# One core: ALiBi and mask move from VectorE into the score matmul group, and float64 weights convert without a clamp

## The chip, the core and the metric

One core of a Trainium2 chip runs the whole program. The metric is the device time of one execution in microseconds; the kernel before took 464.65 us (median of 3 runs, 463.22 to 468.41). The engines are TensorE (PE, with its weight loads as PEld), VectorE (DVE), ScalarE (ACT), GpSimd (POOL) and SyncE (SP), which issues the DMAs. Each works through its own queue in the order in which the program wrote it.

## What is computed

Three blocks follow one another, all in float32 (weights come partly as float64 bits):

```python
# attention: 2 x 8 heads, 768 positions, head width 64, n_global = 8, n_local = 96
scores = scale * q @ k.T
is_global = pos[None, :] < n_global;  is_local = (rel >= 0) & (rel < n_local)     # rel = query - key
dist = where(is_global & ~is_local, n_local, abs(rel))
scores = where(is_global | is_local, scores - slopes[h] * dist, -1e9)
a = exp(scores - scores.max(-1));  a = a / (a.sum(-1) + 1e-9);  x = a @ v         # heads side by side: [2, 768, 512]
# first mixture
theta = x @ w_theta
y = w_tok_r @ (x * cos(theta)) + w_tok_i @ (x * sin(theta));  u = x + y
x2 = u + max(u @ w_ch, 0)
# second mixture
h = max(x2 @ w_in, 0);  c = conv3(h, conv_w) along the positions
out = (h * sigmoid(c)) @ w_out
```

A query tile of 128 positions needs only its own tile of keys, the local keys before it, and the 8 global keys.

## The kernel before, in words

Large products are made from a high part in fp32r and a low part (the rest), three matmuls for one. `hi` (L79 on ScalarE, L83 on VectorE) rounds to the high part, `lo` (L87) makes the low part, `mm` (L90) is every matmul. For the scores, Q high and Q low are two stationary operands against one K whose upper half holds its own low part, so each query tile has two score matmuls.

**Attention loop.** `run_fast` runs 48 groups, three per head, each of a pair of query tiles, as a software pipeline. In step j the program writes `scores` of group j, `softmax` of j-1 (L299), `exps` of j-2 (L308), `transposes` of j-3 (L317), `evacuate` of j-4 (L79, ScalarE) and `pv` of j-5; then come, by step, `table` (L269), the normalisation, the high and low parts of the next head's K and Q, and transposes of finished heads (L416). A query tile's scores are 256 columns: 120 local keys before it, 8 global keys and its own 128; the first tile of a head has only its own 128. Scores of a pair lie in one PSUM bank; the tag S has two such banks. `softmax` is one custom VectorE instruction for each tile: it adds the head's table T (distance times slope, masked entries huge) to the scores in PSUM, scales, writes the sum to an SBUF buffer `sS` and gives the row minimum, which a second small instruction reads out. `exps` then works in place on `sS`, so the bank is free once the custom instructions are done. `table` makes T from the distance table `Dt` anew for each head, two instructions.

**Weights.** Every weight tile is a job of six items in `Net.weight`: load (L117, on SP's queue, into one of two buffers `wst`), `f64_a` (L95, ScalarE, absolute value of the upper words), `f64_b` (L100 clamps in float, L101 shifts and masks in integers, both VectorE), `f64_c` (L107, L108, VectorE), then the high part (L79, ScalarE) and the low part (L87, VectorE). `advance` lists the items of neighbouring jobs in the order low part of n-3, `f64_a` of n-1, `f64_b` and `f64_c` of n-2, load of n, high part of n-2. The loop takes one item per step up to step 32 and three from then on; later stages take up to twelve between groups of matmuls. The jobs are 4 of w_theta (512 columns), 24 of w_tok (384), then 4 of w_ch, 8 of w_in and 8 of w_out (512).

**After attention.** `theta` of batch 0 runs within the last third of the loop, 6 matmuls of 512 columns a step. `reduce_theta` (L456 to L459) scales it on ScalarE, rounds it with the magic number in one VectorE instruction (L458) and subtracts (L459); 12 tiles in all. `trig` (L466 to L472) makes the sine and cosine parts. Then `tail` runs the token matmuls, w_ch, w_in with the convolution and gate, and w_out.

`begin` computes the distance table, the high and low parts of the first head, and a flag that chooses between `run_fast` and a general arm; the scores of group 0 need only the first half of those parts.

Of the kernel before, what the change touches and what calls it, by code (L numbers as in the profile page):

```python
# [21 lines left out]
P = 128  # L22
# [3 lines left out]
NH = B * H  # L26
NG = 8
NPREV = P - NG
# [14 lines left out]
def f32_of_bits(b):  # L43
    return float(np.array([b], np.uint32).view(np.float32)[0])


F64_LOW = f32_of_bits(0x38000000)
F64_HIGH = f32_of_bits(0x47EFFFFF)


class Net:
# [41 lines left out]
    def f64_a(self, w, t):  # L93

        self.nc.scalar.activation(t.bitcast(F32), w[:, 1 : w.shape[1] : 2].bitcast(F32), AF.Abs)  # L95

    def f64_b(self, w, t):

        nc = self.nc
        nc.vector.tensor_scalar(t.bitcast(F32), t.bitcast(F32), F64_LOW, F64_HIGH, op0=ALU.max, op1=ALU.min)  # L100
        nc.vector.tensor_scalar(t, t, 3, 0x3FFFFFFF, op0=ALU.logical_shift_left, op1=ALU.bitwise_and)  # L101

    def f64_c(self, w, t):

        nc = self.nc
        lo, hi = w[:, 0 : w.shape[1] : 2], w[:, 1 : w.shape[1] : 2]
        nc.vector.scalar_tensor_tensor(t, lo, 29, t, op0=ALU.logical_shift_right, op1=ALU.bitwise_or)  # L107
        nc.vector.scalar_tensor_tensor(t, hi, -(1 << 30), t, op0=ALU.bitwise_and, op1=ALU.bitwise_or)  # L108
# [89 lines left out]
class Attention:  # L198


    def __init__(self, net, xs):
# [9 lines left out]
        self.sS = [a2[:, 715 + 512 * i : 715 + 512 * i + 512] for i in range(3)]  # L211
        self.pt = [a0[:, w + vw : w + vw + 512], a1[:, w + vw : w + vw + 512], a2[:, 2251:2763]]
        self.T = [a2[:, 2763:3019], a1[:, SLOT - P :]]
        self.qk = [n.head["qk0"], n.slot("a3", [P, 2 * S + NT * KW], F32R, "qk1")]
# [36 lines left out]
def split_q(net, st, qk, eh, el):  # L251
    q = st[:, 0:S]
    net.hi(eh, qk[:, 0:S], q)
    net.lo(el, qk[:, S : 2 * S], q, qk[:, 0:S])


class FastAttention(Attention):
# [15 lines left out]

    def scores(self, j):
        i, tp = divmod(j, 3)
        net = self.net
        Q, K = self.Q(i), self.K(i)
        sp = net.bank("S", 2)
        for u in range(2):
            t = 2 * tp + u  # L280
            if t == 0:
                o, r = sp[:, P : 2 * P], K[:, 0:P]
            else:
                o, r = sp[:, 256 * u : 256 * u + 256], K[:, KW * (t - 1) + NG : KW * t + P]
            for a in range(2):
                net.mm(o, Q[:, a, t * P : t * P + P], r, a == 0, a == 1)
        self.state[j] = {"sp": sp}

    def softmax(self, j):
        i, tp = divmod(j, 3)  # L290
        nc, net, s = self.nc, self.net, self.state[j]
        sS = self.sS[j % 3]
        nm = net.small.tile([P, 2], F32, tag="nm", name=net.uid("nm"), bufs=3)
        rng = []
        for u in range(2):
            t0 = tp == 0 and u == 0
            c = slice(256 * u + (P if t0 else 0), 256 * u + 256)
            rng.append(c)
# [4 lines left out]
        s["exp"] = (sS, rng, nm)  # L303

    def exps(self, j):
        sS, rng, nm = self.state[j]["exp"]
        for u in range(2):
            self.nc.scalar.activation(sS[:, rng[u]], sS[:, rng[u]], AF.Exp, bias=nm[:, u : u + 1], scale=-1.0)  # L308

    def transposes(self, j):  # L310
# [4 lines left out]
        for u, a in self.chunks(tp):  # L315
            c = slice(256 * u + P * a, 256 * u + P * a + P)
            self.nc.tensor.transpose(pt[:, c], sS[:, c], net.head["ident"])  # L317
# [23 lines left out]
class GeneralAttention(Attention):  # L341


    def unit(self, i, t, o):
# [18 lines left out]
        for hf in range(2):  # L363
# [5 lines left out]
            nc.scalar.activation(s[:, HALF * hf : HALF * hf + HALF], sp[:, 0:HALF], AF.Copy, scale=0.125)  # L369
# [17 lines left out]
class Mix:  # L387
# [64 lines left out]
    def reduce_theta(self, th, out):  # L452
# [3 lines left out]
        nc.scalar.activation(out, th, AF.Copy, scale=1.0 / TWO_PI)  # L456
        yield
        nc.vector.tensor_scalar(t, out, MAGIC, -MAGIC, op0=ALU.add, op1=ALU.add)  # L458
        nc.vector.tensor_tensor(out, out, t, op=ALU.subtract)  # L459

    def trig(self, b, t, r, z, em, eh, el):
# [5 lines left out]
        nc.scalar.activation(r, r, AF.Sin, scale=TURN)  # L467
# [132 lines left out]
    def tail(self, early):  # L600
# [94 lines left out]
        self.wch = [wc[:, c] for c in range(3)] + [wr[:, 0]]  # L695
        src = n.io["w_ch"].rearrange("(c p) n -> c p n", p=P)
# [24 lines left out]
        for step in (n.f64_a, n.f64_b, n.f64_c):  # L721
            step(n.head["cwb"], n.head["cwt"])
# [56 lines left out]
def run_fast(tc, net):  # L779
# [13 lines left out]
    mix.alloc_xTs()  # L793
    NJ = 3 * NH
# [20 lines left out]
    for j in range(NJ + LAG_N + 3):  # L815
# [6 lines left out]
        if tp == 0 and i < NH:  # L822
            att.table(i)
# [108 lines left out]
def begin(nc, io, net, small, head):  # L932
# [9 lines left out]
    cwb = small.tile([P, 2 * NF * 3], I32, name="cwb")  # L942
    nc.sync.dma_start(cwb, io["conv_w"].bitcast(I32))

    R = scratch[:, STAGE : STAGE + 384]
    Dt = small.tile([P, 384], F32, name="Dt")
    nc.gpsimd.iota(R[:, 0:NPREV], pattern=[[-1, NPREV]], base=NPREV, channel_multiplier=1, allow_small_or_imprecise_dtypes=True)
    nc.gpsimd.iota(R[:, NPREV:P], pattern=[[1, NG]], base=0, channel_multiplier=0, allow_small_or_imprecise_dtypes=True)
# [71 lines left out]
```

## Time and profile before

| | |
|---|---|
| median of 3 runs | 464.65 us (463.22 to 468.41) |
| profiled execution, span | 463.6 us |
| busy: PE / PEld / DVE / ACT | 411.5 / 380.5 / 383.3 / 217.6 us |
| instructions | 6488 |
| last chain by engine: DVE / PE / DMA / ACT | 46% / 37% / 7% / 4% |

Busy time is the union of an engine's instructions; a matmul's end is modelled and its record holds the pipeline's latency, so a busy PE can have room left. The granted clock is given as a share of 2.4 GHz: 1.00 is 2.4 GHz and 0.50 is 1.2 GHz. In the rows below L is a line of the kernel before.

### The profile page before, as it was taken

To read this page: it belongs to the slowest core of one execution; us is meant where nothing else is said; L and a number is where in the kernel's file an instruction comes from. 1 tells how busy PE (TensorE), PEld (TensorE's weight loads), DVE (VectorE), ACT (ScalarE), POOL (GpSimd) and SP (SyncE) were. 2 spreads that over 40 slices of the span, in tenths; PEclk is the share of its full clock that TensorE was granted. 3 is DMA by queue.
4 is the path that set the end of the run, shared out by engine and by line. 5 is a ranking of instruction groups with operands and counts; after the bars stand their busy time and mean duration, and the time that the engine had idled before them with its cause. 6 is when DMAs were issued, how large, how long until landed. Compare 5 with 4: busy or idle time off the path is not lost.

```text
span 463.6 us, 6488 instructions
## 1 busy us (share of the span) xinstructions
PE 411.5 (89%) x2376; PEld 380.5 (82%) x2376; DVE 383.3 (83%) x854; ACT 217.6 (47%) x420; POOL 1.4 (0%) x10
## 2 busy tenths in 40 slices
PE   3788778889988999899876999769999999999995
PEld 2777778777877799899765999759999999888885
DVE  5899998999999998898677898899999999991000
ACT  4767765866657731641322323373465454540000
POOL 1000000000000000000000000000000000000000
PEclk9999978999999999999999999979999999999999
DMA  6865554555231002202444343322311000003111
GB/s 231 308 197 201 175 167 152 187 172 171 66 101 35 1 0 69 69 2 68 108 130 125 92 136 105 123 92 60 122 47 47 0 1 0 1 0 136 47 45 52
DMA packets 14296, 44.52 MB, mean 96 GB/s; under 512 B 1840, under 2 KB 2352, under 8 KB 14256
## 3 DMA queue, kind: packets, MB, share of 16 engines
q1 hardware_dynamic: 14256, 44.03, 29.6%
q8 instruction: 20, 0.33, 0.3%
q14 instruction: 20, 0.16, 0.1%
HBM read 40.88 MB, written 3.15 MB: 95 GB/s over the span
## 4 chain that ended last, share of the span: by engine, by line
DVE 46%; PE 37%; DMA 7%; ACT 4%; issue 3%; SPq 0%; ACTq 0%; DVEq 0%
PE O L90 11%; PE S L90 8%; PE PT L90 8%; DVE qk L87 6%; DVE a L299 6%; PE X L90 5%; DVE wbit L107 4%; PE TH L90 4%; DMA wst<-w_tok 3%; DVE wbit L108 3%; DVE z L87 3%; DMA wst<-w_in 3%; DVE wbit L101 2%; DVE wbit L100 2%; DVE qk L83 2%
## 5 line engine op out<-in xcount | busy, mean ns | idle before, releaser
L95 ACT ACTIVATE wbit<-wst 128x512 f32<-128x512 f32 (+1 forms) x48 | 29.3, 615 | 77.1 <-DMA wst<-w_tok 29.9
L90 PE MATMUL S<-qk 128*128 128x256 f32 (+1 forms) x192 | 39.9, 334 | 27.7 <-DVE nm L299 19.8
L90 PEld LDWEIGHTS S<-qk 128*128 128x128 f32 x192 | 30.4, 217 | 34.6 <-DVE nm L299 25.0
L308 ACT ACTIVATE a<-a,nm 128x256 f32<-128x256 f32 (+1 forms) x96 | 42.4, 486 | 28.9 <-DVE nm L299 28.8
L90 PE MATMUL O<-wt,z 128*128 128x384 f32 x144 | 30.1, 345 | 9.5 <-ACT wt L79 9.5
L299 DVE CUSTOM_DVE_ANT_0 a<-S,a 128x256 f32<-128x256 f32 (+1 forms) x96 | 34.4, 397 | 1.6 <-ACT a L308 1.2
L90 PEld LDWEIGHTS O<-wt,z 128*128 128x128 f32 x144 | 24.7, 188 | 13.3 <-ACT wt L79 11.4
L108 DVE SCALAR_TENSOR_TENSOR wbit<-wst,wbit 128x512 int32<-128x512 int32 (+1 forms) x48 | 30.0, 625 | 1.7
L90 PE MATMUL O<-a,a 128*128 128x65 f32 x236 | 31.3, 277 | 0.0
L107 DVE SCALAR_TENSOR_TENSOR wbit<-wst,wbit 128x512 int32<-128x512 int32 (+1 forms) x48 | 30.0, 624 | 1.5
L87 DVE TENSOR_TENSOR qk<-a,qk 64x816 fp32r<-64x816 f32 (+1 forms) x30 | 29.5, 982 | 1.2 <-ACT qk L79 0.3
L90 PEld LDWEIGHTS O<-a,a 128*128 128x128 f32 x236 | 30.4, 201 | 0.0
L317 PE MATMUL PT<-ident,a 128*128 128x128 f32 x176 | 29.8, 292 | 0.6 <-ACT a L79 0.6
L79 ACT ACTIVATE wt<-wbit 128x384 fp32r<-128x384 f32 x24 | 12.4, 518 | 35.0 <-DVE wbit L108 34.9
L79 ACT ACTIVATE a<-PT 128x512 f32<-128x512 f32 (+1 forms) x48 | 26.3, 548 | 1.6 <-PE PT L317 1.5
L90 PE MATMUL TH<-wth,xTs 128*128 128x512 f32 x96 | 26.0, 408 | 0.5 <-ACT r L456 0.2
L90 PE MATMUL PT<-wt,z 128*128 128x384 f32 x132 | 25.8, 335 | 0.0
L87 DVE TENSOR_TENSOR wt<-wbit,wt 128x384 fp32r<-128x384 f32 x24 | 13.3, 556 | 12.7 <-ACT wt L79 12.7
L90 PEld LDWEIGHTS PT<-wt,z 128*128 128x128 f32 x132 | 23.2, 188 | 0.0
L317 PEld LDWEIGHTS PT<-ident,a 128*128 128x128 f32 x176 | 22.4, 151 | 0.7 <-ACT a L79 0.7
L90 PE MATMUL S<-wt,z 128*128 128x384 f32 x120 | 22.3, 337 | 0.5 <-DVE z L87 0.5
L90 PEld LDWEIGHTS S<-wt,z 128*128 128x128 f32 x120 | 20.9, 188 | 0.8 <-DVE z L87 0.8
(188 smaller groups left out, 905.7 us busy)
## 6 DMA issues: line engine op xcount, KB each, us to landing
a<-qk SPq DMA_DIRECT2D x14, 792.0 KB, 5.5
wst<-w_tok SPq DMA_DIRECT2D x24, 384.0 KB, 3.1
a<-v SPq DMA_DIRECT2D x16, 357.5 KB, 3.2
wst<-w_in SPq DMA_DIRECT2D x8, 512.0 KB, 3.5
wst<-w_out SPq DMA_DIRECT2D x8, 512.0 KB, 3.6
out<-scratch SPq DMA_DIRECT2D x11, 256.0 KB, 2.0
wst<-w_theta SPq DMA_DIRECT2D x4, 512.0 KB, 5.4
wst<-w_ch SPq DMA_DIRECT2D x4, 512.0 KB, 3.6
```

What stands on the lines that cost most here:

```text
L79: self.nc.scalar.activation(out, in_, AF.Copy)
L83: self.nc.vector.tensor_copy(out, in_)
L87: e.tensor_tensor(out, in_, hi.bitcast(F32), op=ALU.subtract)
L90: self.nc.tensor.matmul(out, l, r, start=start, stop=stop)
L95: self.nc.scalar.activation(t.bitcast(F32), w[:, 1 : w.shape[1] : 2].bitcast(F32), AF.Abs)
L100: nc.vector.tensor_scalar(t.bitcast(F32), t.bitcast(F32), F64_LOW, F64_HIGH, op0=ALU.max, op1=ALU.min)
L101: nc.vector.tensor_scalar(t, t, 3, 0x3FFFFFFF, op0=ALU.logical_shift_left, op1=ALU.bitwise_and)
L107: nc.vector.scalar_tensor_tensor(t, lo, 29, t, op0=ALU.logical_shift_right, op1=ALU.bitwise_or)
L108: nc.vector.scalar_tensor_tensor(t, hi, -(1 << 30), t, op0=ALU.bitwise_and, op1=ALU.bitwise_or)
L299: nc.vector.tensor_tensor_reduce(sS[:, c], s["sp"][:, c], self.T[1 if t0 else 0], scale=-0.125, scalar=3.0e38, op0=ALU.add, op1=ALU.min, a ...
L308: self.nc.scalar.activation(sS[:, rng[u]], sS[:, rng[u]], AF.Exp, bias=nm[:, u : u + 1], scale=-1.0)
L317: self.nc.tensor.transpose(pt[:, c], sS[:, c], net.head["ident"])
```

## The change

* The table is no longer added by VectorE. `begin` builds one fp32r table of distances (`table`, 464 columns: one 232-column half for a first tile, one for every other), and for each head an identity matrix times its slope (`E`) is the stationary operand of one matmul that opens the score group with the table as moving operand, 464 columns. For all but a head's first group the moving operand reads the same 232 columns twice. Q's parts carry the factor -0.125.
* `softmax` is one `tensor_reduce` with minimum over both tiles of the pair, straight from PSUM. `exps` reads the scores from PSUM and writes `sS`.
* The local keys before a tile are 96 instead of 120: 232 score columns for 256. The transposes still take 128 columns each; the V rows that meet the surplus are zero.
* `f64_a` multiplies by 2^-112 instead of taking the absolute value, `f64_b` is only the shift, `f64_c` takes the sign bit alone.
* `reduce_theta` reads the bank twice on ScalarE and rounds and subtracts in one VectorE instruction.
* The conv_w load moves from `begin` to the place before w_ch's loads, into a corner of `scratch`.

```diff
-NPREV = P - NG
+NPREV = 96
+SKIP = P - NPREV
+PG = NPREV + NG
+RW = PG + P
     def f64_a(self, w, t):
-        self.nc.scalar.activation(t.bitcast(F32), w[:, 1 : w.shape[1] : 2].bitcast(F32), AF.Abs)
+        self.nc.scalar.activation(t.bitcast(F32), w[:, 1 : w.shape[1] : 2].bitcast(F32), AF.Copy, scale=REBIAS)
     def f64_b(self, w, t):
-        nc.vector.tensor_scalar(t.bitcast(F32), t.bitcast(F32), F64_LOW, F64_HIGH, op0=ALU.max, op1=ALU.min)
-        nc.vector.tensor_scalar(t, t, 3, 0x3FFFFFFF, op0=ALU.logical_shift_left, op1=ALU.bitwise_and)
+        self.nc.vector.tensor_scalar(t, t, 3, None, op0=ALU.logical_shift_left)
...
+def scaled(net, eh, el, q, hi, lo):
+    nc = net.nc
+    if eh == "A":
+        nc.scalar.activation(hi, q, AF.Copy, scale=QSCALE)
+    elif eh == "V":
+        nc.vector.tensor_scalar(hi, q, QSCALE, None, op0=ALU.mult)
+    if el:
+        nc.vector.scalar_tensor_tensor(lo, q, QSCALE, hi.bitcast(F32), op0=ALU.mult, op1=ALU.subtract)
...
-    def table(self, i):
-        for t, c in zip(self.T, (slice(0, 256), slice(256, 384))):
-            self.nc.vector.tensor_scalar(t, self.net.head["D"][:, c], -8.0 * 2.0 ** -(i % H + 1), None, op0=ALU.mult)
+    def slope(self, i):
+        self.nc.vector.tensor_scalar(self.eye(i), self.net.head["ident"], 2.0 ** -(i % H + 1), None, op0=ALU.mult)
     def scores(self, j):
+        if tp == 0:
+            net.mm(sp[:, 0 : 2 * RW], self.eye(i), T, True, False)
+        else:
+            net.mm(
+                sp[:, 0 : 2 * RW].rearrange("p (u c) -> p u c", u=2), self.eye(i),
+                T[:, RW:].unsqueeze(1).to_broadcast([P, 2, RW]), True, False,
+            )
             for a in range(2):
-                net.mm(o, Q[:, a, t * P : t * P + P], r, a == 0, a == 1)
+                net.mm(o, Q[:, a, t * P : t * P + P], r, False, u + a == 2)
     def softmax(self, j):
-            nc.vector.tensor_tensor_reduce(
-                sS[:, c], s["sp"][:, c], self.T[1 if t0 else 0],
-                scale=-0.125, scalar=3.0e38, op0=ALU.add, op1=ALU.min, accum_out=nm[:, u : u + 1],
-            )
+        self.nc.vector.tensor_reduce(
+            s["nm"], s["sp"][:, 0 : 2 * RW].rearrange("p (u c) -> p u c", u=2), axis=AX.X, op=ALU.min
+        )
     def exps(self, j):
-            self.nc.scalar.activation(sS[:, rng[u]], sS[:, rng[u]], AF.Exp, bias=nm[:, u : u + 1], scale=-1.0)
+            c = slice(PG if j % 3 + u == 0 else RW * u, RW * u + RW)
+            self.nc.scalar.activation(sS[:, c], s["sp"][:, c], AF.Exp, bias=s["nm"][:, u : u + 1], scale=-1.0)
...
         nc.scalar.activation(out, th, AF.Copy, scale=1.0 / TWO_PI)
-        yield
-        nc.vector.tensor_scalar(t, out, MAGIC, -MAGIC, op0=ALU.add, op1=ALU.add)
-        nc.vector.tensor_tensor(out, out, t, op=ALU.subtract)
+        nc.scalar.activation(t, th, AF.Copy, scale=1.0 / TWO_PI, bias=MAGIC)
+        yield
+        nc.vector.scalar_tensor_tensor(out, t, -MAGIC, out, op0=ALU.add, op1=ALU.subtract)
...
-        if tp == 0 and i < NH:
-            att.table(i)
+        if tp == 1 and i + 1 < NH and (i + 1 < 3 or (i + 1) % H > 2):
+            att.slope(i + 1)
```

`slope(0)` stands in `run_fast` ahead of the loop. In `begin` the table's eight VectorE instructions stand between the first and the second half of the low parts; before, four of its nine stood ahead of them and the rest behind.

## Rows read from the trace of the kernel before

**Rows 1.** The page: length of the profiled execution.
```profile
span 463.6 us, 6488 instructions
```
**Rows 2.** Windows by stage: length, then busy (count) PE, PEld, DVE, ACT, POOL; clock
```profile
23.50:94.40 70.90, 57.33 (x448) 55.21 (x447) 67.58 (x210) 49.79 (x107) 0.00 (x0) 0.93 0.55 182
94.40:143.50 49.10, 43.86 (x291) 37.59 (x290) 46.80 (x140) 31.20 (x68) 0.00 (x0) 1.00 0.37 121
...
168.00:190.00 22.00, 21.41 (x124) 21.08 (x122) 18.64 (x39) 4.23 (x9) 0.00 (x0) 1.00 0.19 54
...
213.00:262.00 49.00, 40.31 (x219) 37.24 (x218) 36.66 (x81) 14.01 (x28) 0.00 (x0) 1.00 0.43 123
262.00:308.00 46.00, 39.55 (x219) 37.51 (x217) 40.74 (x82) 16.33 (x30) 0.00 (x0) 0.98 0.34 104
308.00:392.00 84.00, 84.00 (x468) 84.00 (x469) 81.66 (x123) 43.16 (x78) 0.00 (x0) 0.97 0.15 45
```
**Rows 3.** Waits, 10 to 150 us: the longest of PE, then of DVE.
```profile
PE S L90 <- DVE nm L299: 19.8, 18, 2.1
...
DVE a L299 <- ACT a L308: 1.2, 1, 1.2
```
**Rows 4.** Chain that ended last, in the loop: start, length (us), what
```profile
101.86 0.34 DVE a L299
102.21 0.34 DVE a L299
...
105.64 0.28 DVE wbit L100
...
107.49 0.35 DVE scratch L458
...
108.56 0.20 DVE a L299
```
**Rows 5.** Timeline of one step: start, length (us), engine, instruction
```profile
84.94 0.90 ACT L308 ACTIVATE a<-a,nm 128x256 f32<-128x256 f32 x2
84.94 0.43 DVE L269 TENSOR_SCALAR a<-Dt 128x256 f32<-128x256 f32 x2
```
**Rows 6.** Groups by form, VectorE from PSUM: busy us, mean ns of one
```profile
L519 DVE TENSOR_TENSOR xT<-S,xT 128x384 f32<-128x384 f32 x4 | 2.2, 551 | 0.0
...
L83 DVE COPY scratch<-O 128x512 f32<-128x512 f32 x2 | 1.4, 686 | 10.3 <-PE O L90 10.3
```
**Rows 7.** Chain that ended last, whole span: pieces from later stages
```profile
201.23 1.86 DVE xT L519 x4
...
223.90 3.05 DMA wst<-w_tok
...
230.64 3.06 DMA wst<-w_tok
...
392.54 11.02 PE O L90 x48
```
**Rows 8.** Timeline of PE: two successive score groups in the theta steps
```profile
112.56 0.62 PE L90 MATMUL S<-qk 128*128 128x128 f32 x4
...
115.65 0.63 PE L90 MATMUL S<-qk 128*128 128x256 f32 x4
```
**Rows 9.** Windows of 2 us where the granted clock fell
```profile
62.00:64.00 2.00, 0.20 (x1) 0.20 (x2) 2.00 (x7) 0.56 (x2) 0.00 (x0) 0.88 0.70 199
64.00:66.00 2.00, 2.00 (x11) 2.00 (x11) 1.93 (x8) 1.71 (x5) 0.00 (x0) 0.50 0.70 221
```
**Rows 10.** Windows of L100 alone: length, busy DVE (count), clock, DMA
```profile
213.00:262.00 49.00, 4.90 (x14) 1.00 0.43 123
262.00:308.00 46.00, 4.20 (x10) 0.98 0.34 104
```
**Rows 11.** Timeline of the start: first score matmuls, first table, first custom instruction
```profile
5.73 1.30 PE L90 MATMUL S<-qk 128*128 128x128 f32 x4 [5.73 <-DVE qk L87]
...
9.41 0.43 DVE L269 TENSOR_SCALAR a<-Dt 128x256 f32<-128x256 f32 x2 [0.50 <-issue]
9.99 0.29 DVE L299 CUSTOM_DVE_ANT_0 a<-S,a 128x128 f32<-128x128 f32 x1 [0.15 <-DVE a L269]
```

More of the change, by code (lines that the diff above doesn't have):

```diff
@@ L40 @@
 LAG_SM, LAG_EXP, LAG_T, LAG_EV, LAG_PV, LAG_N = 1, 2, 3, 4, 5, 6
[L43 to L48, printed above, removed]
+REBIAS = 2.0 ** -112
+QSCALE = -0.125
 class Net:
@@ L210, in __init__ @@
         self.v = [a0[:, w : w + vw], a1[:, w : w + vw], a2[:, 0:vw]]
[L211 to L214, printed above, removed]
+        self.sS = [a2[:, vw + 2 * RW * i : vw + 2 * RW * (i + 1)] for i in range(3)]
+        x = vw + 6 * RW
+        self.pt = [a0[:, w + vw : w + vw + 512], a1[:, w + vw : w + vw + 512], a2[:, x : x + 512]]
+        a3 = n.slot("a3", [P, SLOT], F32R, "qk1")
+        self.qk = [n.head["qk0"], a3[:, 0 : 2 * S + NT * KW]]
+        y = 2 * S + NT * KW
+        self.E = [a3[:, y + P * i : y + P * i + P] for i in range(5)]
         self.xs = xs
@@ L276, in scores @@
         net = self.net
-        Q, K = self.Q(i), self.K(i)
+        Q, K, T = self.Q(i), self.K(i), net.head["table"]
         sp = net.bank("S", 2)
+        if tp == 0:
[5 more added lines that the diff above has]
+            )
         for u in range(2):
@@ L316, in transposes @@
             c = slice(256 * u + P * a, 256 * u + P * a + P)
-            self.nc.tensor.transpose(pt[:, c], sS[:, c], net.head["ident"])
+            self.nc.tensor.transpose(pt[:, c], sS[:, self.columns(u, a)], net.head["ident"])
         s["pt"] = pt
@@ L566, in gate @@
         nc, n = self.nc, self.net
-        cw = n.head["cwt"].bitcast(F32).rearrange("p (f k) -> p f k", k=3)
+        cw = self.cwt.bitcast(F32).rearrange("p (f k) -> p f k", k=3)
         for hf in range(2):
@@ L695, in tail @@
         self.wch = [wc[:, c] for c in range(3)] + [wr[:, 0]]
+        self.cwb, self.cwt = (n.head["scratch"][:, x : x + w].bitcast(I32) for x, w in ((2432, 48), (2480, 24)))
+        nc.sync.dma_start(self.cwb, n.io["conv_w"].bitcast(I32))
         src = n.io["w_ch"].rearrange("(c p) n -> c p n", p=P)
@@ L721, in tail @@
         for step in (n.f64_a, n.f64_b, n.f64_c):
-            step(n.head["cwb"], n.head["cwt"])
+            step(self.cwb, self.cwt)
         pipe = Pipe()
@@ L793, in run_fast @@
     mix.alloc_xTs()
+    att.slope(0)
     NJ = 3 * NH
@@ L985, in begin @@
     nc.vector.tensor_scalar(nnl, nl, -1.0, None, op0=ALU.mult)
-    cwt = small.tile([P, NF * 3], I32, name="cwt")
-    head.update(scratch=scratch, qk0=qk0, D=Dt, ident=ident, half_pi=hp[:, 0:1], ng=ng, nl=nl, nnl=nnl, flag=fi, cwb=cwb, cwt=cwt)
+    head.update(scratch=scratch, qk0=qk0, table=table, ident=ident, half_pi=hp[:, 0:1], ng=ng, nl=nl, nnl=nnl, flag=fi)
 def kernel(q, k, v, n_global, n_local, moe_w_theta, moe_w_tok_r, moe_w_tok_i, moe_w_ch, moe2_w_in, moe2_conv_w, moe2_w_out):
```

76 lines of the change are left out of this document (38 added, 38 removed).

## The prediction, written before the result

> **What bounds the kernel now.** I read the page first for the span, 463.6 us [rows 1], then the windows by stage, then the waits, then the chain that ended last, and single steps in the timeline. In the attention loop VectorE sets the pace: it is busy 67.58 of 70.90 us between 23.5 and 94.4 us, and 46.80 of 49.10 us from there to 143.5, where theta runs along [rows 2]. The waits agree. PE stood 19.8 us for the minimum that L299 makes, while VectorE's longest wait in the same stretch is 1.2 us [rows 3]. PE is not far behind, though: 57.33 and 43.86 us busy [rows 2]. From 168 to 213 us PE is nearly full (21.41 of 22.00 us in the first half) and VectorE works next to it. From 213 to 308 us neither is full; there the weight jobs run as a loop, load, ScalarE, VectorE, next load, one turn for two weights: the loads on the chain start at 223.90 and 230.64, 6.74 us apart [rows 7]. From 308 us on PE is full and sets the end [rows 2], so nothing saved on VectorE there counts.
>
> **The bias on PE.** A pair of tiles costs VectorE two custom instructions and their readouts, 0.34 and 0.34 us on the chain, so about 0.69; a head's first pair costs 0.20 and 0.34, 0.54 [rows 4]. The two table instructions take 0.43 [rows 5]. A head: 2 x 0.69 + 0.54 + 0.43 = 2.35 us.
>
> In their place stands a minimum over 464 columns from PSUM, and the trace has no reduction. The nearest rows are a 384-column VectorE read of PSUM of 551 ns and a 512-column one of 686 ns, 1.05 ns a column, and four of the former follow at 1.86 / 4 = 0.465 us [rows 6, 7]. So 464 columns are 0.465 + 80 x 1.05 ns = 0.55 us. That is the lower bound too, since no row reads PSUM faster; the upper is two passes over the columns, 1.03. I take 0.55, because custom and ordinary instructions alike keep that rate in the rows. The slope instruction, 128 columns, is the smaller part of the table pair, 0.2, and is needed 13 times (three heads of batch 1 find theirs kept from batch 0). A head: 3 x 0.55 + 0.2 x 13 / 16 = 1.81. The saving is 0.54 us a head, 0.18 a pair.
>
> The Trainium skill (VectorE: DVE Perf Modes, Rules for kernel authors) speaks against this part: it calls `tensor_reduce` the slowest Vector operation, runs it at its base rate only and advises restructuring around it. The base rate is what the PSUM rows show; if slowest meant more than that, the sum would go by the fourth rival. No run here shows a reduction yet.
>
> **What PE pays.** One opening matmul of 464 columns for each of 48 groups. 384-column matmuls come at most every 84.00 / 468 = 0.18 us [rows 2], 512-column ones every 11.02 / 48 = 0.23 [rows 7]; between them, 0.21 at full clock, double at half. Lower bound 0.18. The moving operand that reads 232 columns twice has no row; the upper bound is the 0.42 of half clock. The narrower score matmuls save nothing: a group with two 128-column matmuls lasts 0.62 us, one with four of 256 lasts 0.63 [rows 8], so the width is not what they wait for.
>
> **By stretch.** From 23.5 to 94.4 us lie 27 pairs and 5 clamps. A clamp (L100) costs 0.28 on the chain and 0.02 to the next [rows 4], 0.30; the 512-column ones some 0.1 more. VectorE loses 27 x 0.18 + 1.8 = 6.7 and comes to 64.2 us. PE comes to 57.33 + 27 x 0.21 = 63.0. So VectorE still leads, by little; I take -6.0 (bounds -6.7 and 0).
>
> From 94.4 to 143.5 us there are 14 pairs (2.5 us), 7 clamps (2.1) and six roundings of theta, L458, 0.35 + 0.02 each (2.2): VectorE falls by 6.8 to 42.3. PE comes to 43.86 + 14 x 0.21 = 46.8, and the groups, 3.09 us apart when theta fills PE [rows 8], would be 3.30. PE takes over; -2.3 (bounds -6.8 and +1).
>
> At the start there is a loss. Group 0's scores began at 5.73 us and the first custom instruction at 9.99 [rows 11]; now they wait for E, which VectorE makes where the first table instruction stood, at 9.41. Behind it come the opening matmul, 0.4 at half clock, and the four scores, 1.30 [rows 11]: the first minimum starts at 9.4 + 0.2 + 1.7 = 11.3, 1.3 us later, and I take 1.5 because the second S bank comes free later too. The first two heads give back 5 pairs x 0.18: +0.6 (bounds 0 and +2).
>
> **After attention.** 168 to 213 us: three L458 lie on the chain and one just before, 4 x 0.37, and four clamps, 1.2; against them a second ScalarE read, some 0.5 by the 0.90 of two exponentials [rows 5], on the way to the first sine of batch 1. That is -2.2, of which I count -1.8: PE is full here, so VectorE only runs ahead and gains where PE stands later, between 213 and 308 us, 8.7 + 6.5 us [rows 2]. 213 to 262 us: 14 clamps [rows 10], one in two on the loop's path, 7 x 0.30 = -2.1. 262 to 308 us: 10 clamps of 0.42 [rows 10]; where VectorE itself is the chain each counts, where the load is, one in two, so seven: -2.9 (bounds for the three stretches together 0 and -10, every clamp counted). Behind 308 us: 0.
>
> **Edits at no cost.** `f64_a`, the mask in `f64_c` and the scaling of Q replace an instruction by one of the same passes. Moving conv_w's load shortens SP's queue at the start, where the next loads wait for the flag anyway; in its new place it goes ahead of w_ch's loads, is 48 words wide, and the scratch corner's last user finished in batch 1's trig; were that late, all of w_ch would wait behind it. The second read in `reduce_theta` holds the only TH bank some 0.5 us longer, six times, in the stretch where I already let PE lead.
>
> **The bank.** A wait is added: an S bank is freed by the exponentials, not by the custom instruction. If scores j+2 wait, transposes of j-1 and `pv` of j-3 wait behind them on PE, and the evacuation behind those. From minimum to freed bank are 0.55 + 0.90, then 0.85 to the next scores' end by the 0.62 of a group and the new matmul [rows 5, 8]: 2.3 us, against two steps of 2.4 to 3.3. It is covered unless ScalarE has 2.5 us of other work ahead of the exponentials.
>
> **Sum.** -6.0 - 2.3 + 0.6 - 1.8 - 2.1 - 2.9 = -14.5; 463.6 - 14.5 = 449.1 us of span. The median of the runs was 1.05 us above this execution's span: 450 us.
>
> **Rivals.** (1) PE does not take over: its records contain pipeline latency, so the theta steps too shorten as VectorE does: attention -12.9, the tail as before: 463.6 - 12.9 - 6.8 + 1.05 = 445. For it: theta's groups are the only stretch with PE at 9 tenths. If the half-clock stretch behind the PE pause at 62 to 64 us [rows 9] also goes, two or three less, 442.
> (2) PE or the bank eats the attention gain whole: each step must lose 0.18 us. For it: the 63.0 against 64.2 us above. Against: every PE wait in the rows is for VectorE. Only the tail is left: 463.6 + 0.6 - 6.8 + 1.05 = 458.
> (3) The clamps were covered, by loads and by PE: only attention, 463.6 - 7.7 + 1.05 = 457. For it: the 3.05 us load in every turn of the loop; against: it and VectorE follow one another.
> (4) The reduction needs two passes: 48 x 0.48 = +23.0, VectorE's loop 23 - 13.5 = 9.5 longer, PE no longer near: 463.6 + 9.5 + 1.5 - 6.8 + 1.05 = 469. It undoes the gain of attention from 0.83 us a reduction on.
> (5) The opening matmul runs as a slow form, 0.8 us or more: 57.33 + 27 x 0.8 = 79 and 43.86 + 14 x 0.8 = 55 us: +8 and +6, in all 473. Against: its operands are of the scores' type, and a group of those lasts 0.63 us.
>
> **How the numbers follow.** The forecast 0.46, rival 1 0.20, rival 2 0.14, rival 3 0.07, rival 4 0.06, rival 5 0.04, anything else 0.03. The range from 441 to 460 us holds the first four, about 0.85 with something lost at its edges. A change over 1%, about what a measurement of this kernel can tell, means under 460.0 or over 469.3 us: faster 0.81 (the first four, less what lies close to 460), within 1% 0.12, slower 0.07.
>
> **What would show it.** A reduction line of about 0.63 us, 48 times, and no L100; pairs in the loop 0.2 us closer; PE's wait for the minimum smaller and one for the exponentials in its place; the loop of two weights 6.4 us instead of 6.74. The forecast is wrong if reductions last 0.9 us or more, if VectorE stands for scores in most steps, or if the loads come as far apart as before.

## The result, and the profile after

The changed kernel takes 443.45 us (median of 3 runs, 443.0 to 451.74) against 464.65 (463.22 to 468.41): a ratio of 0.952 [0.945, 0.960], 21 us less. The forecast was 450, its range 441 to 460. The profiled execution of after spans 441.2 us, that of before 463.6 [rows 1].

The page of after: the span, the busy time of the engines, and the group of the new reduction (busy us, mean ns of one | idle before, releaser).

```profile
span 441.2 us, 6455 instructions
PE 410.4 (93%) x2424; PEld 383.6 (87%) x2424; DVE 349.8 (79%) x631; ACT 218.5 (50%) x432; POOL 1.4 (0%) x10
...
L314 DVE TENSOR_REDUCE nm<-S 128x2 f32<-128x464 f32 x48 | 30.5, 635 | 3.4 <-PE S L89 3.4
```

The reduction is there 48 times at 635 ns; the forecast had said "about 0.63". VectorE stood 3.4 us ahead of all of them together, for scores. It is busy 349.8 us in all, 383.3 before.

Windows of after by stage (length, then busy time and count of PE, PEld, DVE, ACT, POOL; granted clock, DMA share, GB/s). The first two are the loop without theta and with it, the answer to the first two of [rows 2]; the third lies in the matmuls with the token weights, the fourth runs from there to the end of w_ch, and the last is the stage in which PE was full before.

```profile
24.00:89.00 65.00, 58.47 (x466) 55.51 (x465) 60.69 (x113) 47.39 (x107) 0.00 (x0) 0.97 0.56 198
89.00:127.00 38.00, 37.83 (x260) 34.17 (x259) 35.11 (x73) 28.62 (x65) 0.00 (x0) 1.00 0.46 146
...
183.00:241.00 58.00, 52.07 (x281) 49.61 (x280) 44.06 (x90) 18.83 (x37) 0.00 (x0) 0.97 0.31 90
241.00:303.00 62.00, 60.42 (x348) 60.10 (x347) 55.95 (x112) 25.42 (x48) 0.00 (x0) 1.00 0.37 111
303.00:370.00 67.00, 67.00 (x384) 67.00 (x384) 64.51 (x87) 35.64 (x62) 0.00 (x0) 1.00 0.12 37
```

VectorE still leads ahead of theta (60.69 of 65.00 against PE's 58.47); with theta PE has become full (37.83 of 38.00, VectorE 35.11). For the fourth the kernel before needs a window cut at the same matmuls, 255.48 to 325.35 us; that of after is 241.53 to 302.82:

```profile
255.48:325.35 69.87, 63.42 (x344) 61.38 (x343) 63.63 (x130) 25.97 (x50) 0.00 (x0) 0.95 0.35 105
```

```profile
241.53:302.82 61.29, 59.72 (x344) 59.40 (x343) 55.27 (x111) 25.42 (x48) 0.00 (x0) 1.00 0.37 108
```

For the same 344 matmuls PE is busy 3.7 us less and idle 1.6 us instead of 6.5.

The waits in the loop of after, 9 to 132 us (us in total, times, longest), to be read against [rows 3]:

```profile
PE S L89 <- DVE qk L280: 8.8, 1, 8.8
PE S L89 <- ACT a L322: 5.2, 11, 1.4
...
DVE nm L314 <- PE S L89: 3.4, 3, 1.7
```

PE's 19.8 us for the minimum are gone; 5.2 us for the exponentials stand in their place, and the 8.8 at the start, for the first slope.

To see where the 21 us went I cut both profiled executions at the same matmuls. In this table "theta" is the first matmul of theta, "S1" the first of batch 1's theta, "token" the first with the token weights, "X" the end of the last of them that writes the tile X, which closes the third of four passes, "w_ch" the end of the last matmul with w_ch, all in us from the start of the execution. The fourth token pass lies behind X; it takes 26.1 us in both.

| | theta | S1 | token | X | w_ch | end of the last matmul |
|---|---|---|---|---|---|---|
| before | 94.4 | 153.1 | 167.9 | 255.5 | 325.3 | 458.8 |
| after | 89.7 | 142.6 | 157.9 | 241.5 | 302.8 | 436.3 |
| gained up to here | 4.7 | 10.5 | 10.0 | 13.9 | 22.5 | 22.4 |
| forecast, summed | 5.4 | 7.7 | 7.7 | 11 to 12 | 14.5 | 14.5 |

So the loop without theta gave a little less than forecast, the loop with theta 5.8 us where 2.3 were forecast, and the stages from the token weights to the end of w_ch 12.5 where 6.8 were (157.5 us before, 144.9 after). Behind w_ch, where PE was full, 133.4 us became 133.5: nothing, as forecast. From S1 to token 0.5 us was lost, 14.8 to 15.3; the four kernels here with the old rounding of theta take 14.8 in this stretch, and all with the new one, whose bank is read twice on ScalarE, 15.3. The prediction had put that read at some 0.5.

### The profile page after: what moved, and what is told of

It is laid out like the page before. It is cut to its first block, busy times and chain, and to the rows that moved or that the text cites. A ratio compares the mean times of both kernels' runs of the same rounds, so it can differ in the third digit from the quotient of the medians.

```text
span 441.2 us, 6455 instructions
## 1 busy us (share of the span) xinstructions
PE 410.4 (93%) x2424; PEld 383.6 (87%) x2424; DVE 349.8 (79%) x631; ACT 218.5 (50%) x432; POOL 1.4 (0%) x10
## 4 chain that ended last, share of the span: by engine, by line
PE 48%; DVE 31%; DMA 9%; ACT 7%; issue 4%; SPq 0%; ACTq 0%; DVEq 0%
PE O L89 13%; PE S L89 12%; PE PT L89 8%; PE TH L89 8%; PE X L89 5%; DMA wst<-w_tok 4%; DVE wbit L104 3%; DVE z L86 3%; DVE wbit L105 3%; DVE qk L86 2%; DVE nm L314 2%; DVE qk L262 2%; PE PT L331 2%; DVE wbit L98 2%; DVE z L82 2%
## 5 line engine op out<-in xcount | busy, mean ns | idle before, releaser
L322 ACT ACTIVATE a<-S,nm 128x232 f32<-128x232 f32 (+1 forms) x96 | 37.2, 446 | 24.0 <-DVE nm L314 21.3
L89 PE MATMUL S<-table,qk 128*128 128x464 f32 x48 | 23.0, 480 | 17.0 <-DVE qk L280 8.8
L89 PEld LDWEIGHTS S<-qk 128*128 128x128 f32 x192 | 31.7, 207 | 2.6 <-DVE qk L262 0.7
L314 DVE TENSOR_REDUCE nm<-S 128x2 f32<-128x464 f32 x48 | 30.5, 635 | 3.4 <-PE S L89 3.4
L89 PEld LDWEIGHTS O<-wt,z 128*128 128x128 f32 x144 | 25.8, 194 | 8.5 <-ACT wt L78 7.2
L89 PE MATMUL S<-qk 128*128 128x232 f32 (+1 forms) x192 | 32.1, 292 | 0.5 <-DVE qk L262 0.5
L89 PE MATMUL O<-a,a 128*128 128x65 f32 x236 | 30.4, 272 | 0.0
L78 ACT ACTIVATE a<-PT 128x512 f32<-128x512 f32 (+1 forms) x48 | 27.4, 571 | 2.5 <-PE PT L331 2.5
L89 PEld LDWEIGHTS S<-table,qk 128*128 128x128 f32 x48 | 9.7, 202 | 21.6 <-ACT a L322 11.7
L331 PE MATMUL PT<-ident,a 128*128 128x128 f32 x176 | 28.3, 282 | 0.0
L78 ACT ACTIVATE wt<-wbit 128x384 fp32r<-128x384 f32 x24 | 12.5, 522 | 21.0 <-DVE wbit L105 21.0
```

The lines of the kernel that those rows point to most:

```text
L78: self.nc.scalar.activation(out, in_, AF.Copy)
L89: self.nc.tensor.matmul(out, l, r, start=start, stop=stop)
L314: self.nc.vector.tensor_reduce(s["nm"], s["sp"][:, 0 : 2 * RW].rearrange("p (u c) -> p u c", u=2), axis=AX.X, op=ALU.min)
L322: self.nc.scalar.activation(sS[:, c], s["sp"][:, c], AF.Exp, bias=s["nm"][:, u : u + 1], scale=-1.0)
L331: self.nc.tensor.transpose(pt[:, c], sS[:, self.columns(u, a)], net.head["ident"])
```

## The experiments

Each run's median stands beside a median of the kernel before on the same chip (464.3 to 465.2 us in the three sets), and the ratio with its interval. For stages I use the intervals of the table above.

### One part undone, or one part alone

**old_f64**: the changed kernel with the conversion of before.

```diff
-        self.nc.vector.tensor_scalar(t, t, 3, None, op0=ALU.logical_shift_left)
+        nc.vector.tensor_scalar(t.bitcast(F32), t.bitcast(F32), F64_LOW, F64_HIGH, op0=ALU.max, op1=ALU.min)
+        nc.vector.tensor_scalar(t, t, 3, 0x3FFFFFFF, op0=ALU.logical_shift_left, op1=ALU.bitwise_and)
```

> The changed kernel (443.45 us) with the old float64 conversion put back: absolute value, clamp (L100 of before, 48 times) and the old mask; everything else as changed. The changed kernel came out 22.4 us of span shorter, some 9 us of it between 281 and 325 us of the old time axis, where I had reckoned 2.9. Theory A: the clamps held the weight conversion behind PE there; with them back the stalls of PE ahead of w_in (6 us) and the half clock that follows them return, and the time is 455 to 458 us. Theory B: the stalls went because attention ended earlier and the weight pipeline had a better start, whatever the clamps do; then only the terms reckoned for clamps come back, 2 to 3 in attention and 5 in the tail, 449 to 452 us, and PE keeps its 2.4 GHz at the start of w_in.

Measured: 460.55 us, ratio 0.988 [0.979, 0.996], above the range of either theory. The half clock is back ahead of w_in, 300.7 to 307.5 us of its profiled execution, as theory A said; theta begins there at 95.5 us instead of 89.7.

**f64_alone**: the kernel before with `f64_a`, `f64_b` and `f64_c` of after, the same edit the other way round.

> The kernel before (464.65 us) with the new float64 conversion alone: 48 clamps gone, nothing else. Theory A (clamps held the tail back): -3.5 us in attention, where VectorE sets the pace, and -10 to -12 behind it: 449 to 452 us. Theory B: -3.5 and -5: 455 to 457 us, with the PE stalls and the half clock ahead of w_in still there.

Measured: 452.56 us, 0.973 [0.965, 0.981]. The time is near theory A's; but the half clock of theory B is still there, 296.3 to 303.2 us of its profiled execution, behind 2.4 us in which PE stood.

**old_theta**: the changed kernel with the rounding of before.

```diff
-        nc.scalar.activation(t, th, AF.Copy, scale=1.0 / TWO_PI, bias=MAGIC)
         yield
-        nc.vector.scalar_tensor_tensor(out, t, -MAGIC, out, op0=ALU.add, op1=ALU.subtract)
+        nc.vector.tensor_scalar(t, out, MAGIC, -MAGIC, op0=ALU.add, op1=ALU.add)
+        nc.vector.tensor_tensor(out, out, t, op=ALU.subtract)
...
```

(Further down the scale of the sine changes its sign with it.)

> The changed kernel (443.45 us) with the old rounding of theta: one ScalarE read of the bank, rounding and subtraction as two VectorE instructions (12 more on VectorE, 12 fewer on ScalarE). By my sum PE sets the pace while theta runs, so the six of batch 0 cost nothing and the ones of batch 1 that lie on VectorE's path ahead of full PE nothing or 1.5: 443 to 445 us. If VectorE still set the pace (rival 1), 6 x 0.37 and 4 x 0.37 come back: 447 us.

Measured: 449.09 us, 0.965 [0.958, 0.972], above what either case allowed.

**bias_alone**: both of these edits in the changed kernel, so that of the change the bias on PE, the minimum, the 232 columns and the moved load are left.

> The kernel before with the score part of the change alone (opening matmul, one minimum for a pair, 232 columns, and the place of the conv_w load): old float64 conversion, old rounding of theta. By my sum VectorE loses 0.18 us a pair, 8.6 us in all, less what PE takes over while theta runs (2.5 of the 14 pairs there) and a start 0.5 us later: 457 to 459 us. If the gains add up, it is the changed kernel plus what the two kernels that put one part back add. If the opening matmul and the bank held by ScalarE eat the gain (rival 2), 463 to 466 us.

Measured: 459.87 us, 0.989 [0.982, 0.995], a little above the range for gains that add up.

What follows. The stages tell the parts apart, in us; a smaller number is a gain.

| | theta to S1 | token to X | X to w_ch | token to w_ch |
|---|---|---|---|---|
| before | 58.7 | 87.6 | 69.9 | 157.5 |
| bias_alone | 55.3 | 87.8 | 69.6 | 157.4 |
| f64_alone | 60.7 | 84.0 | 65.4 | 149.3 |
| old_f64 | 53.9 | 85.5 | 69.8 | 155.2 |
| old_theta | 53.3 | 84.0 | 64.3 | 148.2 |
| after | 52.9 | 83.6 | 61.3 | 144.9 |

The bias gives 3.4 us where theta runs along and nothing behind attention (157.4 against 157.5). The conversion gives its time behind attention: 8.2 us alone, 10.3 in the changed kernel (155.2 to 144.9). With the rounding 3.3 go there (148.2 to 144.9), 3.0 of them between X and w_ch; but two_openings, below, which has all instructions of after in this stretch, takes 146.7, so an effect of this size in single executions isn't shown to be the rounding's own. The conversion is thus the largest part of the change; by the fastest runs of the three edits, 458.7 with the bias alone, 449.4 with the conversion alone, 446.3 against 443.0 for the rounding, the parts are 4.1, 13.5 and 3.3 us, where the fastest run of before took 462.9: 21 in sum, and 20 for the whole. By the medians the bias gives 4.4 and the conversion 11.8. In the table, f64_alone's 60.7 from theta to S1 holds a half-clock stretch, 139 to 150 us, which no other of these has.

The loop of two weights is on the chain of each of these. bias_alone:

```profile
212.92 3.14 DMA wst<-w_tok
...
219.62 3.04 DMA wst<-w_tok
```

The kernel after:

```profile
203.48 3.05 DMA wst<-w_tok
...
209.70 3.03 DMA wst<-w_tok
```

One turn is 6.70 us with the clamp and 6.22 without; it was 6.74 in the kernel before [rows 7], and the forecast said 6.4.

old_theta's 449.09 us are more than the 3.3 of the tail explain. In its profiled execution theta begins at 92.5 us instead of 89.7, in a stage whose instructions are those of after. That part is no effect of the rounding; the next run shows what it is.

### The changed kernel once more

**again**: no edit.

> The changed kernel once more, unchanged, as the base for the other kernels of this set: 443 to 447 us.

Measured: 446.48 us (443.15 to 456.91), 0.953 [0.944, 0.961]: close to the ratio of the first result. In its profiled execution theta begins at 93.9 us, 4.2 later than in the first, and from there on the two agree: 52.9 and 52.9 from theta to S1, 145.2 and 144.9 from token to w_ch. Most of the 4.2 us was lost in a single head. One score group of four matmuls, twice in the first execution of after:

```profile
16.83 1.03 PE L89 MATMUL S<-qk 128*128 128x232 f32 x4
...
19.73 0.61 PE L89 MATMUL S<-qk 128*128 128x232 f32 x4
```

and twice in again:

```profile
30.96 1.03 PE L89 MATMUL S<-qk 128*128 128x232 f32 x4
...
36.29 0.60 PE L89 MATMUL S<-qk 128*128 128x232 f32 x4
```

A group lasts 1.03 us at the lower level of the clock and 0.61 at the higher one; PE came up to the higher one before 20 us in the one execution and between 31 and 36 in the other. The head in which it happened took 10.8 us in again (first minimum at 26.09, the next head's at 36.86) and 7.0 in after (24.72 to 31.68). So a profiled execution can be 4 us or more off ahead of theta for the same program, and I compare stages behind theta, or medians.

### Which conversions count

**clamp_early** and **clamp_late**: the old conversion for w_theta and w_tok only, the first 28 jobs, or for w_ch, w_in and w_out only.

```diff
         box = {}
+        self.count = getattr(self, "count", 0) + 1
+        old = self.count <= 28
```

(`> 28` for clamp_late; `old` chooses between the two forms of `f64_a`, `f64_b`, `f64_c`.)

> The changed kernel with the old conversion (clamp and masks) for the first 28 weight jobs, w_theta and w_tok, the new one for w_ch, w_in and w_out. Theory A (a clamp costs where its job is late, and the stall ahead of w_in comes from the late jobs): +3.9 in attention and +3 to +4 up to the end of w_tok, the stall ahead of w_in stays away: 449 to 452 us. Theory B (the late stages only inherit how far ahead the pipeline starts): most of the 13 to 17 us that all clamps cost comes back: 454 to 458 us.

> The changed kernel with the old conversion for the last 20 weight jobs alone, w_ch, w_in and w_out; 10 to 12 of them run while PE works on the token matmuls and w_ch. Theory A: those clamps cost 0.42 each on VectorE, and the stall of PE ahead of w_in with its half clock comes back: +6 to +9, 450 to 453 us. Theory B: +0 to +3, 444 to 447 us, PE's waits between 255 and 305 us stay below 3 us.

Measured: clamp_early 450.47 us, 0.966 [0.959, 0.972]; clamp_late 451.97 us, 0.972 [0.963, 0.980]: both theory A. From token to w_ch clamp_early takes 148.5 us (3.6 more than after), clamp_late 151.5 (6.6 more, all of it from X to w_ch, 68.0 against 61.3). The early clamps thus cost 3.6 and the late ones 6.6 of the conversion's 10.3. Ten of the late clamps fell into the window of before from 262 to 308 us, 4.2 us of VectorE in all [rows 10], and the 6.6 are more than that. The rest is seen at the first matmuls of batch 1, in windows of 2 us of clamp_late:

```profile
288.00:290.00 2.00, 0.68 (x3) 0.19 (x1) 1.90 (x5) 1.77 (x5) 0.00 (x0) 0.74 0.00 0
290.00:292.00 2.00, 0.73 (x2) 0.73 (x3) 2.00 (x5) 1.69 (x4) 0.00 (x0) 0.50 0.37 80
```

The same place in the kernel before, windows which stand in no row above:

```profile
306.00:308.00 2.00, 0.00 (x0) 0.00 (x0) 1.97 (x5) 1.35 (x3) 0.00 (x0) 0.50 0.00 0
308.00:310.00 2.00, 2.00 (x6) 2.00 (x7) 2.00 (x5) 1.86 (x5) 0.00 (x0) 0.50 0.84 260
```

In both PE stands still while VectorE is full, the granted clock falls to 0.50, the lower level, and PE then works on at it: 6 matmuls in the 2 us from 308, where it is full. In the execution of after, 278 to 290 us, PE is busy 10.43 of 12.00 and the clock stays at 1.00. PE's waits at this place, 240 to 310 us (us in total, times, longest), in clamp_late:

```profile
PE O L97 <- DVE us L94: 3.9, 3, 2.2
```

and in after:

```profile
PE O L89 <- DVE us L86: 1.6, 1, 1.6
```

So a late VectorE is paid for twice: 3.9 us of standing instead of 1.6, and behind it some us at half clock. In the kernel before a run of 14 matmuls at 308.00 us lasts 4.84 us on the chain, 0.35 each, where 384-column matmuls at full clock come every 0.18 [rows 2].

The clamps lengthen the stop, but they are not its only cause. From X to w_ch the profiled executions divide by the granted clock: with 3.4 to 7.4 us of half clock in that stretch it took 69.9 us in before, 69.6 in bias_alone, 69.8 in old_f64, 68.0 in clamp_late, 65.4 in f64_alone and 64.3 in old_theta; without, 63.0 in clamp_early, 60.9 in again and 61.3 in after. f64_alone and old_theta have no clamp there.

### Who leads in the loop

**two_openings**: the opening matmul issued twice, the second time added to the first, so the bias counts double. **two_reduces**: the minimum computed twice.

```diff
+            net.mm(sp[:, 0 : 2 * RW], self.eye(i), T, False, False)
...
```
```diff
+        self.nc.vector.tensor_reduce(
+            s["nm"], s["sp"][:, 0 : 2 * RW].rearrange("p (u c) -> p u c", u=2), axis=AX.X, op=ALU.min
+        )
```

> The changed kernel with the opening matmul of each group issued twice, so that the bias counts double (the scores are not the reference's). 48 more matmuls of 464 columns on PE and nothing else. If PE sets the pace while theta runs, as I reckoned, the 15 groups there cost 0.21 each, 3.2 us; before that PE has about 6 us of room in 65 and VectorE leads, so the 30 groups cost 0 to 3: 4 to 6 us in all, 448 to 450. If VectorE leads all over, 0 to 2 us: 444 to 446. If PE leads all over, 48 x 0.21 to 0.3: 10 to 14 us, 454 to 458.

> The changed kernel with the minimum of each pair taken twice: 48 more reductions on VectorE, 0.55 us each by their pitch, 26 us in all; the output is the same. If VectorE leads up to the start of theta, 30 of them cost 0.55 each, 16 us, in that stretch; while theta runs VectorE is idle some 5 us in 37, so the 15 there cost 2 to 4: 18 to 21 us in all, 462 to 465, about where the kernel before stood. If PE leads all over, less than 10 us.

Measured: two_openings 448.99 us, 0.962 [0.954, 0.970]; two_reduces 470.61 us, 1.013 [1.004, 1.023]. The stages ahead of theta and with theta, two_openings:

```profile
24.00:93.00 69.00, 65.01 (x520) 62.08 (x519) 63.32 (x117) 49.61 (x112) 0.00 (x0) 1.00 0.52 188
93.00:131.00 38.00, 38.00 (x253) 34.21 (x251) 33.48 (x69) 28.49 (x64) 0.00 (x0) 1.00 0.46 145
```

two_reduces:

```profile
30.00:109.00 79.00, 64.06 (x455) 60.93 (x456) 75.71 (x136) 47.98 (x107) 0.00 (x0) 0.89 0.47 163
109.00:157.00 48.00, 44.06 (x291) 38.21 (x291) 45.91 (x90) 30.95 (x70) 0.00 (x0) 1.00 0.37 122
```

Twice the work on PE lengthens the stretch from theta to S1 by 2.1 us (52.9 to 55.0), eleven steps in it by 2.2 or 0.20 each, and a period of two heads ahead of theta by 0.3 (14.3 to 14.6), though six openings went into each. So PE leads with theta; ahead of it, even doubled, it only draws level (65.01 against 63.32 us busy). Twice the work on VectorE lengthens two heads from 14.3 to about 18.1, and theta to S1 by 6.4 (to 59.3): VectorE leads again (45.91 of 48.00 against PE's 44.06). The total grew more than expected. Two reductions one behind the other stand 0.66 us apart:

```profile
100.06 0.63 DVE L314 TENSOR_REDUCE nm<-S 128x2 f32<-128x464 f32 x1
100.72 0.64 DVE L317 TENSOR_REDUCE nm<-S 128x2 f32<-128x464 f32 x1
```

which is their full duration and 0.03 more, and makes 48 x 0.66 = 32 us instead of 48 x 0.55 = 26. Ahead of theta it is 30 x 0.66 = 19.8 us, and theta begins 19.4 us later than in after (109.1 against 89.7). The mean granted clock of the first window is 0.89, with half-clock stretches at 36 to 43, 77 to 83 and 94 to 97 us, but they cost nothing that shows where VectorE leads: two heads around the second took 18.10 us (73.30 to 91.40), the two heads before them, at full clock, 18.24.

**cols208**: 72 keys ahead of a tile instead of 96, thus 416 columns in all three of matmul, minimum and exponentials.

```diff
-NPREV = 96
+NPREV = 72
...
```

> The changed kernel with 72 local keys before a tile instead of 96, 208 score columns for 232 (the keys 73 to 95 back are left out of the softmax, so the output is not the reference's). If the width is worth nothing to the score matmuls, their pitch stays at 0.11 us and only the reduction (48 columns, 0.05 us) and the opening (0.02) shorten: two heads take 14.0 for 14.3 us up to theta, 1.5 to 2 us in all. If PE pays by columns, 0.01 us a matmul more and 3 to 4 us in all.

Measured: 445.49 us (439.82 to 456.58), 0.944 [0.934, 0.953], not told from after by the median. Two heads take 14.0 us instead of 14.3, and the reduction

```profile
L314 DVE TENSOR_REDUCE nm<-S 128x2 f32<-128x416 f32 x48 | 28.1, 585 | 7.4 <-PE S L89 7.4
```

is 50 ns shorter for 48 columns, 1.04 ns a column. Six of these are 0.3 us, as much as the period is shorter. VectorE leads there, so this period can't tell what the matmuls' width is worth; with theta, where PE leads, it can. Eleven steps took 36.86 us there (100.34 to 137.20) against 37.21, 0.03 a step, of which the shorter opening has 0.02; and score matmuls of 208 and of 232 columns start 0.11 us apart alike (111 and 112 ns in the median of these steps). That leaves next to nothing for their width.

### The order of the weight jobs

The waits of before behind attention, 145 to 464 us, are for pieces of weight jobs:

```profile
PE O L90 <- ACT wt L79: 9.5, 6, 2.5
PE O L90 <- DVE us L87: 4.0, 3, 2.4
PE TH L90 <- DVE xT L519: 2.1, 1, 2.1
```

After, 132 to 440 us, the first two are shorter, the third gone:

```profile
PE O L89 <- ACT wt L78: 5.9, 4, 2.1
PE O L89 <- DVE us L86: 1.6, 1, 1.6
```

**order_hl**: what is left of PE's waits is for `wt`, the last two steps of a job, so these are put ahead of the next job's first ones.

```diff
-        put(n - 3, 5)
-        put(n - 1, 1)
         put(n - 2, 2, 3)
         put(n, 0)
         put(n - 2, 4)
+        put(n - 1, 1)
+        put(n - 2, 5)
```

> The changed kernel with the items of the weight jobs in another order: conversion of n-2, load of n, high part of n-2, first ScalarE step of n-1, low part of n-2 (before: low part of n-3, first ScalarE step of n-1, conversion of n-2, load of n, high part of n-2). The high and low part then run while the load is on its way instead of between its landing and the next conversion. If the turn of the loop (load, ScalarE, VectorE, next load) sets the pace behind attention, a turn of two weights falls from 6.2 to 5.2 us and PE's 5.9 us of waits for converted w_tok go: 436 to 440 us. If PE or the transfers set it, within 1 us of the changed kernel; in attention VectorE then waits for ScalarE's high part and may lose 1 to 2 us.

Measured: 444.13 us, 0.952 [0.945, 0.959], where after stood at 0.953 in the same set. From token to X it is 7.6 us shorter (76.0 against 83.6), with no load of w_tok on the chain any more, yet the total is the same: nearer the second of the cases expected. PE's longest waits, 130 to 460 us:

```profile
PE O L89 <- DVE us L86: 3.0, 2, 2.4
PE TH L89 <- DVE xT L533: 1.0, 1, 1.0
PE O L89 <- ACT wt L78: 0.9, 2, 0.6
```

`wt` fell from 5.9 to 0.9, and `us` rose from 1.6 to 3.0. Windows of 2 us there:

```profile
284.00:286.00 2.00, 0.36 (x2) 0.37 (x3) 2.00 (x5) 1.32 (x3) 0.00 (x0) 1.00 0.29 47
286.00:288.00 2.00, 1.39 (x6) 1.07 (x5) 2.00 (x6) 1.93 (x5) 0.00 (x0) 0.60 0.58 219
288.00:290.00 2.00, 2.00 (x8) 2.00 (x7) 2.00 (x6) 0.98 (x3) 0.00 (x0) 0.50 0.00 0
```

It is the picture of clamp_late: X to w_ch takes 67.4 us instead of 61.3, and 6.1 of the 7.6 are given back. (The next expectation, from a less exact cut at X, says 6.5 and 5.) In the loop, where the same order holds, two heads take 15.0 us instead of 14.3.

**late_order**: the new order only from the head of `tail` on, and in the w_ch loop three pieces a step for batch 1 and one for batch 0.

```diff
...
+        n.late = True
...
-                    n.run(2)
+                    n.run(3 if b else 1)
```

> The changed kernel with the other order of the weight items (conversion, load, high part, next ScalarE step, low part) from the token matmuls on alone, and with one weight item a group instead of two while batch 0 goes through w_ch, three instead of two for batch 1. The order as a whole took 6.5 us out of the token stage and gave 5 back ahead of batch 1 of w_ch, where VectorE worked on weights before the split that PE waited for, and the half clock followed. If that was the cause, attention stays as in the changed kernel, the token stage is 5 to 6 us shorter and w_ch not longer: 436 to 440 us. If VectorE's work as a whole sets that point, the time stays within 2 us of the changed kernel's.

Measured: 439.59 us (436.96 to 444.86), 0.941 [0.933, 0.949], the fastest of all these kernels. Token to w_ch takes 138.1 us against 144.9, and PE's longest waits, 130 to 460 us, are down to these:

```profile
PE TH L90 <- DVE xT L541: 1.1, 1, 1.1
PE O L90 <- ACT wt L79: 0.9, 2, 0.6
PE O L90 <- DVE us L87: 0.8, 2, 0.6
```

Between 282 and 294 us the granted clock stays at 1.00. The interval overlaps a little with that of after in the other set, [0.944, 0.961]; the 6.8 us of the stage are the surer sign. The gain to X is kept, 76.0 us as in order_hl, and X to w_ch takes 62.1, near the 61.3 of after. The run makes two edits there, the order kept for the tail alone and the other pieces a step, and does not tell which of them kept the stop away.

## Why the prediction was right

**Direction and size.** 443.45 us lies in the range, 6.5 under the forecast. Of the mechanisms, that VectorE leads ahead of theta, PE with theta, the weight loop behind attention and PE alone at the end, all four are borne out. Two terms of the sum were too small, and one came near by two misses that cancel.

**The reduction: right.** 635 ns, 1.04 ns a column. In the loop it is followed after 0.55 us by an instruction of another kind, the price in the sum. Timeline of after:

```profile
52.85 0.63 DVE L314 TENSOR_REDUCE nm<-S 128x2 f32<-128x464 f32 x1
53.40 0.22 DVE L280 TENSOR_SCALAR qk<-ident 128x128 fp32r<-128x128 f32 x1
```

So the fourth rival, two passes, did not come. The Trainium skill (VectorE: DVE Perf Modes, Rules for kernel authors) calls `tensor_reduce` the slowest Vector operation, at its base rate only. The base rate is what was measured here, and it is also the rate of the ordinary PSUM reads of [rows 6], so from PSUM nothing was lost by the choice.

**The opening matmul: right.** In the theta steps, two groups of after:

```profile
94.82 0.37 PE L89 MATMUL S<-table,qk 128*128 128x464 f32 x1
95.03 0.61 PE L89 MATMUL S<-qk 128*128 128x128 f32 x4
...
98.39 0.38 PE L89 MATMUL S<-table,qk 128*128 128x464 f32 x1
98.60 0.61 PE L89 MATMUL S<-qk 128*128 128x232 f32 x4
```

The scores follow 0.21 us behind the opening, the forecast's figure. Ahead of theta, where PE often stood first, they follow after 0.29 us or more, 0.315 in the median of the 21 groups from 40 to 90 us; there VectorE led, and it did not reach the pace. The first of these openings reads 464 columns in a row, the second 232 columns twice; they take the same. The fifth rival (0.8 us) fell with it, and the two score groups, 0.61 both, though two of the four matmuls of the first have 128 columns, bear out that narrower scores save nothing.

**The loop ahead of theta: right.** The fifth and sixth head together took 15.84 us before, 15.41 with the new conversion alone and 14.31 after, between the first minima of the heads; the bias is 1.1 of it, 0.18 for each of six pairs, which is the forecast's saving. Theta in the profiled executions began 4.7 us earlier, forecast 5.4; the time at which the clock came up blurs this by as much.

**The start: near the forecast by luck.** Timeline of after, to be read against [rows 11]:

```profile
8.48 0.22 DVE L280 TENSOR_SCALAR qk<-ident 128x128 fp32r<-128x128 f32 x1
8.84 0.73 PE L89 MATMUL S<-table,qk 128*128 128x464 f32 x1 [8.84 <-DVE qk L280]
...
10.44 0.64 DVE L314 TENSOR_REDUCE nm<-S 128x2 f32<-128x464 f32 x1 [1.75 <-PE S L89]
```

The first minimum starts at 10.44, 0.45 later than before's first instruction and not 1.3: the slope was made at 8.48 and not at 9.41, since what stands ahead of it on VectorE ended 0.35 us earlier and the 0.50 us that VectorE then stood in before [rows 11] did not come back. But the 0.9 us that the first two heads were to give back did not come either: the third head's first minimum starts at 24.72 us in after and 24.25 in before, still 0.47 later, where the sum had +0.6. The clock rose before 20 us in the one and near 23 in the other, which blurs this.

**With theta: PE took over, as forecast, but more was gained.** The failed step is the -2.3, which held PE's 46.8 us against the 49.10 of a window. The first and the last but one of the 13 score groups stand 40.47 us apart before (97.15 to 137.62) and 37.21 after (91.56 to 128.77): -3.3, or 3.68 to 3.38 for a group, near the 3.30 that was forecast for a full PE. What was wrong is the other side: the window of before ended at 143.5, four us behind the last group, and the stage goes on to 153.1. Ahead of the first of these groups and behind the last but one the remaining 2.5 us were gained, 2.7 to 1.8 and 15.5 to 13.9; for 143.5 to 153.1 us the sum had no term. By the runs the bias has 3.4 of the 5.8 and the two other edits together 2.4; taken back one at a time, the conversion costs 1.0 and the rounding 0.4.

**Behind attention: the mechanism was right, the size was off.** -6.8 was forecast and -12.5 measured, more than the -10 of every clamp counted. The term that failed is the -2.9 for 262 to 308 us: from X to w_ch 8.6 us were gained, 4.9 of them by less idle time of PE and 3.7 by shorter busy time for the same matmuls. The sum counted VectorE's instructions; it had no price for PE's waits for `us` and `xT`, which the clamps lengthen, nor for the half clock behind them. Both are in the trace of before (the waits and windows above); the prediction looked at the clock in the loop alone [rows 9] and put that into a rival. clamp_late shows that the late clamps alone bring stop and half clock back; f64_alone, without any clamp, has the half clock still and a stop of 2.4 us, and is 4.5 us shorter there than before. From token to X 4.0 us were gained where some 3.9 were forecast.

**The bank: right.** PE waits 5.2 us in the loop for the exponentials, 11 times, but VectorE's waits for scores are 3.4 us in all; the wait does not reach the pace.

**Rivals.** The first has the time that came, 445 or 442, but not its reason: PE is full with theta. The half clock that before has from 63.5 us shows in after from 77.0 to 80.4, and in again, the same program, not at all. The second and third (458, 457) were the times if the loop or the tail gave nothing. f64_alone, 452.56, and bias_alone, 459.87, stand 6 to 9 and 13 to 16 us above the two medians of after, so each half brought its own.

**Open.** What of old_theta's 449.09 is the rounding: 3.3 us are in the tail of its profile, where an execution with the tail of after was 1.8 longer too; the rest may be the spread of the start. The step from 256 to 232 columns and the place of the conv_w load were not tried alone. Open is also what besides the clamps brings the stop ahead of batch 1 of w_ch, and what sets when PE first comes to the higher level.

## What to carry to other kernels

Moving an addition from the leading engine into a matmul that opens the accumulation pays for as long as the other engine has room; count that room in the steps in which it is scarcest, and to the end of the stage rather than of a window. An instruction that is saved ahead of a wait of PE can be worth more than its own duration, where, as here, the clock falls behind the wait: look for the stop and the half clock in the same place. And when an order is changed to remove one stop, look for the next one before the gain is believed; here 6.1 of 7.6 us came back some 50 us later.

## What the runs showed of the hardware

PE first came to the higher clock at very different times in nearly the same code: before 20 us in the profile of after, near 23 in before, between 31 and 36 in again, and in late_order only between 41 and 47:

```profile
41.40 1.03 PE L90 MATMUL S<-qk 128*128 128x232 f32 x4
...
47.10 0.60 PE L90 MATMUL S<-qk 128*128 128x232 f32 x4
```

Each head like that cost 3.8 us (10.8 against 7.0). The profiled execution of late_order had two of them and was the slowest of its four, 444.86 us against 436.96 to 440.75. The profile's granted clock reads 1.00 in these stretches, so there the level is read from the durations alone. A score group with two matmuls of 128 columns among its four and one with four of 232 took the same 0.61 us, as those with 128 and 256 had before [rows 8]. A moving operand that reads 232 columns twice costs what 464 in a row cost. And two reductions into the same result stand 0.66 us apart, where one followed by another instruction takes 0.55.
